# Third chunk of single batches made on ScalarE and its queue; the raw rows' fill moved to the first tap

## The chip, the cores and the metric

The kernel runs on one core of a Trainium2 chip. The core's engines work side by side and each executes its own instructions in order: TensorE (PE; weight loads are listed as PEld), VectorE (DVE), ScalarE (ACT), GpSimd (POOL) and SyncE (SP). The last three also issue DMA transfers, each from a queue of its own. The metric is the device time of one execution in microseconds, lower is better; the median of several runs is compared.

## The reference

For 8 batches of 4096 tokens with 192 features, a causal convolution with 7 softmax taps (one set per head of 24 features), then a token-mixing and a channel-mixing MLP, each with a residual:

```
w = softmax(weight)                                   # 8 heads x 7 taps
x[b,s,h,g] = sum_k w[h,k] * x_pad[b,s+k,h,g]          # 6 zero rows ahead of each batch
h  = relu(xT @ w_tok1) @ w_tok2                       # over the tokens: 4096 -> 256 -> 4096
u  = x + hT
out = u + relu(u @ w_ch1) @ w_ch2                     # over the features: 192 -> 1536 -> 192
```

Everything is float32. The kernel gets its products by splitting a factor into a high part, rounded to the matmul's format, and a low part, the rest.

## The kernel before

**Groups and tiles.** The batches run in five groups: batch 0, batch 1, then the pairs 2 and 3, 4 and 5, 6 and 7. A batch is eight tiles of 512 tokens. For each tile `mix2` makes u, the convolution's output plus the token mix; then the channel MLP runs in two halves, `channel1` (products with w_ch1, line 1228) and `channel2` (products with w_ch2, lines 1308 and 1309, then the sums into osb, lines 1314 and 1315). After each pair of products of `channel1`, ScalarE writes the relu's high part hh (line 1271) and VectorE its low part hl (line 1272); the next products of `channel2` need both.

**The hand-over of a tile.** `channel1` needs the tile's u with features on the partitions. In the two single batches `transposed_once` does that for the next tile, in the middle of `channel2` of the present one. 192 features are three chunks of 64 features; each tile has its two token halves on the two halves of the 128 partitions, and the tile's pieces are dealt so that TensorE's transposes fill two of three chunks (c = 0 and 1) of each half, one PSUM tile of 128x512 each. ScalarE copies such a tile to own_hi (line 1156), and VectorE subtracts the copy from the same PSUM tile and writes own_lo (line 1157). The third chunk of a partition half is a copy of one of the other half's chunks, so four transfers of 128 KB, issued by GpSimd, carry it across the partitions: two for own_hi and then two for own_lo (lines 1159 and 1160). `channel1` multiplies the chunks 0 and 1 first, high and low parts, and the third chunk's last:

```
prods = [(w, v, c) for cs in (range(ND - 1), [ND - 1]) for w, v in order for c in cs]
```

`transposed_once` runs 14 times, for the tiles 1 to 7 of batch 0 and 0 to 6 of batch 1, between 112 and 564 us. The pairs of batches use other functions.

**Work of later batches.** Beside that runs stage 1 of the groups to come. `load` fetches raw rows of x on SP's queue and, for the first tile of a batch (q2 = 0), fills the 6 rows ahead of it with zeros on GpSimd (line 809). `taps` makes the convolution head by head: the first tap is ScalarE's and writes xc (line 817), the other six are VectorE's and add to it (line 819). xc goes to xcd in DRAM from GpSimd's queue (line 853). For batch 0's second token weights, ScalarE casts the decoded weights to stage (line 1432), and SP stores them to t2d (line 1434); the buffer of stage must be stored before it is written again.

**What sets the order.** The program is written out once, and each engine executes in the order of writing. An object `bg` holds streams of stage-1 work; the foreground's calls of `bg.fg(pe, dve)` tell it the cost of what was just written, and it places as much stage-1 work between as its estimates allow. Waits between engines are set by a framework that follows the tiles which instructions read and write.

Of the kernel before, what the change touches and what calls it, by code (L numbers as in the profile page):

```python
# [142 lines left out]
def conv_mixer_kernel(ctx: ExitStack, tc: tile.TileContext, x, weight, w_tok1, w_tok2, w_ch1, w_ch2, out):  # L143
    nc = tc.nc
# [10 lines left out]
    ND = D // D2  # L155
# [5 lines left out]
    HALO = K - 1  # L161
# [8 lines left out]
    def f32(ap):  # L170
        return ap.bitcast(F32)
# [612 lines left out]
    def stage1(gi, pools):  # L784
# [13 lines left out]
        def load(q2, part):  # L798

            ds = slice(part * DH, (part + 1) * DH)  # L800
            raw = pools(part).tile([P, RB + HALO, nb, DH], F32, name=f"raw{part}")
            for i, b in enumerate(bs):

                at = (b * S + q2 * ST - HALO) * D + ds.start
                assert at >= 0
                src = bass.AP(tensor=x.tensor, offset=x.offset + at, ap=[[RB * D, P], [D, RB + HALO], [1, DH]])
                nc.sync.dma_start(out=raw[:, :, i, :], in_=src)
                if q2 == 0:
                    nc.gpsimd.memset(raw[0:1, 0:HALO, i, :], 0.0)
            return raw  # L810

        def conv(raw, xc, h, k):
# [26 lines left out]
        def taps(q2, h, k):  # L839
            st = states[q2]  # L840
            if k == 0 and h == 0:
                if done.get(("storing", q2 - 2)):
                    bg.release()
                st["xc"] = pools(q2 % 2).tile([P, RB * nb, D], F32, name=f"xc{q2 % 2}")
            for i in range(2):
                conv(st["raw", h // HH], st["xc"], h + i, k)

# [298 lines left out]
    def transposed_once(u):  # L1146

        own = own_tile("hi"), own_tile("lo")
        low, high = slice(0, D2), slice(D2, P)
        for c in range(ND - 1):  # L1150
            ps = ps_x.tile([P, TT], F32, name="ps_x")
            for j in range(TJ):
                cols = u[:, j].rearrange("p c b d -> p (c b d)")[:, c * D2:(c + 2) * D2]
                nc.tensor.transpose(out=ps[:, j * P:(j + 1) * P], in_=cols, identity=ident)
            bg.fg(440, 600)
            nc.scalar.copy(out=own[0][:, c], in_=ps)
            nc.vector.tensor_tensor(out=own[1][:, c], in0=ps, in1=f32(own[0][:, c]), op=ALU.subtract)
        for k in range(2):
            nc.gpsimd.dma_start(out=f32(own[k][high, ND - 1]), in_=f32(own[k][low, 0]))
            nc.gpsimd.dma_start(out=f32(own[k][low, ND - 1]), in_=f32(own[k][high, ND - 2]))  # L1160
        return [(own, own, [range(ND), [(c + 1) % ND for c in range(ND)]])]

    def blocks_sent(z, place):

# [137 lines left out]
    def channel2(i, h, u, osb, js, at=None):  # L1302
        for j in js:
            ts = slice(j * P, (j + 1) * P)
            ps = ps_x.tile([P, TT], F32, name="ps_x")
            for n, f in enumerate(order):
                z = n == NF - 1
                nc.tensor.matmul(out=ps[:, :2 * D], lhsT=h["hh", f][:, ts], rhs=w2[:, f, :], start=n == 0, stop=False)  # L1308
                nc.tensor.matmul(out=ps[:, :D], lhsT=h["hl", f][:, ts], rhs=w2[:, f, :D], start=False, stop=z)  # L1309
                if n % 4 == 3:  # L1310
                    bg.fg(1140, 660 if z else 0, 200)
                if at and at[0] == (j, n):
                    at[1]()
            nc.vector.tensor_tensor(out=rows(osb[:, j]), in0=rows(ps[:, :D]), in1=tokens(u, i)[:, j], op=ALU.add)
            nc.vector.tensor_tensor(out=osb[:, j], in0=ps[:, D:2 * D], in1=osb[:, j], op=ALU.add)  # L1315
# [133 lines left out]
    for gi, bs in enumerate(GROUPS):  # L1449
# [13 lines left out]
        for q in range(NT):  # L1463
            nxt = (gi, q + 1) if q + 1 < NT else (gi + 1, 0)
            for i, b in enumerate(bs):
# [73 lines left out]
                if ahead:  # L1539
                    product2(i, h, u, osb, half[0])  # L1540
                if turn and not pairs and ahead:
                    abc = transposed_once(loaded[1])
                run_ahead(gi)
                if last and q + 1 == NT and i + 1 == nb:
                    for j in range(TJ):
                        if j in half[1]:
                            channel2(i, h, u, osb, [j])
                        store_out(gi, b, q, osb, range(j, j + 1), nc.sync)
                else:
                    if ahead:  # L1550
                        if turn and pairs:
                            made = []
                            channel2(i, h, u, osb, half[1], ((half[1][0], 7), lambda: made.extend(parted(other[:, 1], other))))
                            abc = made
                        else:
                            product2(i, h, u, osb, half[1])
                    else:
                        made = []
                        first_channel2(u, osb, [3], (NF // 3, lambda: made.extend(transposed(loaded[1]))))
                        abc = made  # L1560
                        second_split()
                        first["parted"] = 0.0
                        bg.dve = max(bg.dve, bg.pe) + 6e3

                    store_out(gi, b, q, osb, range(TJ), nc.gpsimd if ahead else nc.scalar)
# [38 lines left out]
```

## Time and profile before

| | us |
|---|---|
| median of 3 runs | 2014.27 |
| lowest and highest of them | 2013.43, 2015.42 |
| profiled execution, its own time | 2013.42 |
| span of the profile | 2011.7 |
| TensorE busy | 1999.8 |
| VectorE busy | 1507.3 |
| ScalarE busy | 749.1 |
| GpSimd busy | 241.6 |

The span is what the profiler recorded, from the first to the last instruction; the execution's own time has 1.7 us around it. Busy times are sums over one engine's instructions, so they lie beside each other in time. A start time in the trace is counted from the beginning of the span.

### The profile page before, as it was taken

How to read it: one execution, taken by the hardware profiler on the slowest of the kernel's cores; microseconds unless marked ns; L12 is line 12 of the kernel's file. 1: busy time of each engine (PE TensorE's matmuls, PEld its weight loads, DVE VectorE, ACT ScalarE, POOL GpSimd, SP SyncE). 2: the span in 40 equal slices, each digit the busy share in tenths (PEclk: the TensorE clock that was granted, in tenths of full speed). 3: DMA queues.
4: the chain of work that ended last, by engine and by line, in shares of the span. 5: the costliest groups of instructions: out<-in, count | busy, mean ns of one | idle time of the engine just before them, and what ended most of it. 6: DMA issues, size and time to landing. Idle time of an engine off the chain costs nothing.

```text
span 2011.7 us, 45407 instructions
## 1 busy us (share of the span) xinstructions
PE 1999.8 (99%) x19007; PEld 1856.2 (92%) x19007; DVE 1507.3 (75%) x3022; ACT 749.1 (37%) x1252; POOL 241.6 (12%) x431
## 2 busy tenths in 40 slices
PE   9999999999999999999999999999999999999999
PEld 9899989998999999999999999999999999999998
DVE  6899989999559999757888789456666666666664
ACT  6666433433333343323334433333233322333322
POOL 1010111111111101111101110111111110111110
PEclk9999999999999999999999999999999999999999
DMA  9957456664454467425346544533323222333310
GB/s 305 307 169 230 147 174 198 191 178 159 149 157 131 141 181 204 149 65 139 76 135 176 153 119 122 139 87 85 85 61 80 75 64 64 84 85 85 85 48 17
DMA packets 284481, 266.61 MB, mean 133 GB/s; under 512 B 190980, under 2 KB 232516, under 8 KB 284276
## 3 DMA queue, kind: packets, MB, share of 16 engines
q1 hardware_dynamic: 258404, 172.85, 30.7%
q0 software_dynamic: 25344, 90.47, 15.1%
q8 instruction: 150, 2.46, 0.5%
q14 instruction: 55, 0.45, 0.1%
q10 hardware_dynamic: 528, 0.39, 0.1%
HBM read 147.25 MB, written 71.30 MB: 109 GB/s over the span
## 4 chain that ended last, share of the span: by engine, by line
PE 92%; DMA 3%; DVE 2%; ACT 1%; SPq 1%; issue 0%; POOL 0%; POOLq 0%; ACTq 0%; DVEq 0%
PE ps_x L1228 38%; PE ps_x L1289 26%; PE ps_x L1308 10%; PE ps_x L1309 5%; PE ps_x L1110 3%; PE ps_a L925 2%; PE ps_a L926 2%; PE ps_a L927 2%; PE ps_x L1080 1%; PE ps_a L921 1%; PE ps_x L1083 1%; DMA x<-in_x_dram 1%; DMA t1d<-kept_t 1%; PE ps_x L1085 1%; PE ps_x L1084 1%; DMA dec_raw<-in_moe_w_tok_dram 1%
## 5 line engine op out<-in xcount | busy, mean ns | idle before, releaser
L1271 ACT ACTIVATE hh<-ps_x 128x512 fp32r<-128x512 f32 x756 | 410.4, 596 | 859.8 <-PE ps_x L1228 859.8
L1272 DVE SCALAR_TENSOR_TENSOR hl<-ps_x,hh 128x512 fp32r<-128x512 f32 x756 | 484.2, 683 | 177.6 <-ACT hh L1271 176.7
L1289 PE MATMUL ps_x<-w,hh 64*128 64x384 f32 x3648 | 523.3, 355 | 0.0
L1289 PE MATMUL ps_x<-w,hl 64*128 64x192 f32 x3648 | 460.7, 247 | 0.0
L1228 PE MATMUL ps_x<-other,w_hi 64*128 64x512 f32 x1728 | 448.3, 388 | 0.1
L819 DVE SCALAR_TENSOR_TENSOR xc<-raw,cw,xc 128x384 f32<-128x384 f32 (+1 forms) x768 | 388.3, 559 | 11.9 <-ACT xc L817 11.8
L1289 PEld LDWEIGHTS ps_x<-w,hl 64*128 64x128 f32 x3648 | 355.8, 188 | 1.8 <-DVE hl L1272 0.3
L1228 PE MATMUL ps_x<-own_hi,w_hi 64*128 64x512 f32 x1440 | 348.0, 392 | 3.6 <-DVE osb L1315 2.0
L1289 PEld LDWEIGHTS ps_x<-w,hh 64*128 64x128 f32 x3648 | 349.7, 184 | 1.4
L1308 PE MATMUL ps_x<-w,hh 128*128 128x384 f32 x1200 | 348.2, 361 | 0.0
L1228 PEld LDWEIGHTS ps_x<-other,w_hi 64*128 64x128 f32 x1728 | 315.7, 184 | 31.8 <-DVE hl L1272 0.4
L1228 PE MATMUL ps_x<-own_lo,w_hi 64*128 64x512 f32 x1440 | 341.7, 387 | 1.3 <-DMA own_lo<-own_lo 1.3
L1228 PE MATMUL ps_x<-own_hi,w_lo 64*128 64x512 f32 x1440 | 341.8, 387 | 0.0
L1309 PE MATMUL ps_x<-w,hl 128*128 128x192 f32 x1200 | 300.6, 250 | 0.0
L1228 PEld LDWEIGHTS ps_x<-own_hi,w_hi 64*128 64x128 f32 x1440 | 214.2, 184 | 33.6 <-issue 6.6
L1228 PEld LDWEIGHTS ps_x<-own_lo,w_hi 64*128 64x128 f32 x1440 | 218.7, 184 | 26.4 <-DMA own_lo<-own_lo 1.7
L1228 PE MATMUL ps_x<-other,w_lo 64*128 64x512 f32 x864 | 242.1, 387 | 0.0
L1228 PEld LDWEIGHTS ps_x<-own_hi,w_lo 64*128 64x128 f32 x1440 | 218.7, 184 | 25.0
L1309 PEld LDWEIGHTS ps_x<-w,hl 128*128 128x128 f32 x1200 | 229.6, 191 | 0.0
L1308 PEld LDWEIGHTS ps_x<-w,hh 128*128 128x128 f32 x1200 | 225.3, 188 | 0.5 <-DVE hl L1272 0.4
L1297 DVE TENSOR_TENSOR osb<-ps_x,osb 128x192 f32<-128x192 f32 x456 | 162.9, 357 | 26.4
L1228 PEld LDWEIGHTS ps_x<-other,w_lo 64*128 64x128 f32 x864 | 159.2, 184 | 16.4
(187 smaller groups left out, 2016.8 us busy)
## 6 DMA issues: line engine op xcount, KB each, us to landing
raw<-in_x_dram SPq DMA_DIRECT2D x56, 672.0 KB, 7.6
t<-t2d SPq DMA_DIRECT2D x64, 512.0 KB, 5.4
out_dram<-osb POOLq DMA_DIRECT2D x62, 384.0 KB, 4.3
xcd<-xc POOLq DMA_DIRECT2D x28, 768.0 KB, 8.4
u<-xcd SPq DMA_DIRECT2D x56, 384.0 KB, 5.7
t<-t1p SPq DMA_DIRECT2D x32, 512.0 KB, 5.9
other<-own_hi POOLq DMA_DIRECT2D x24, 384.0 KB, 3.9
other<-own_lo POOLq DMA_DIRECT2D x24, 384.0 KB, 3.8
```

What stands on the lines that cost most here:

```text
L819: nc.vector.scalar_tensor_tensor(out=dst, in0=src, scalar=cw[:, h, k:k + 1], in1=dst, op0=ALU.mult, op1=ALU.add)
L925: nc.tensor.matmul(out=ps, lhsT=wh, rhs=xh, start=a, stop=False)
L926: nc.tensor.matmul(out=ps, lhsT=wh, rhs=xl, start=False, stop=False)
L927: nc.tensor.matmul(out=ps, lhsT=wl, rhs=xh, start=False, stop=z)
L1110: nc.tensor.matmul(out=ps[:, :n], lhsT=t2[ks, kc, r, j, :], rhs=h1[ks, kc, v, :n], start=m == 0, stop=m == len(prods) - 1)
L1228: nc.tensor.matmul(out=ps, lhsT=w1[w][rows, chunks[h][c], p * P:(p + 1) * P], rhs=t[h][v][rows, c], start=n == 0, stop=n == len(prods) - 1,)
L1271: nc.scalar.activation(out=h["hh", f], in_=ps, func=AF.Relu)
L1272: nc.vector.scalar_tensor_tensor(out=h["hl", f], in0=ps, scalar=0.0, in1=f32(h["hh", f]), op0=ALU.max, op1=ALU.subtract)
L1289: nc.tensor.matmul(out=ps[:, :m], lhsT=h[part, f][ks, ts], rhs=w2[ks, f, :m], start=n == 0 and part == "hh", stop=z and part == "hl",)
L1297: nc.vector.tensor_tensor(out=osb[:, j], in0=v, in1=osb[:, j], op=ALU.add)
L1308: nc.tensor.matmul(out=ps[:, :2 * D], lhsT=h["hh", f][:, ts], rhs=w2[:, f, :], start=n == 0, stop=False)
L1309: nc.tensor.matmul(out=ps[:, :D], lhsT=h["hl", f][:, ts], rhs=w2[:, f, :D], start=False, stop=z)
```

## The change

Three things change. First, in `transposed_once` ScalarE copies the third chunk's part of own_hi out of PSUM: after each chunk's subtraction a copy of 64 partitions by 512, from one partition half of the PSUM tile to the other half of own_hi. Secondly, the two transfers that carry the third chunk's part of own_lo are put into a function `rest`, which `channel2` calls after product n = 7 of its second half's first column block, and they are issued from ScalarE's queue. GpSimd issues none of the four transfers any more. Thirdly, the fill of the raw rows leaves `load` and stands in `taps`, directly ahead of ScalarE's first tap of each half of the heads, and fills both batches of a pair at once.

```diff
@@ load
                 nc.sync.dma_start(out=raw[:, :, i, :], in_=src)
-                if q2 == 0:
-                    nc.gpsimd.memset(raw[0:1, 0:HALO, i, :], 0.0)
             return raw
@@ taps
+            if k == 0 and q2 == 0 and h % HH == 0:
+                nc.gpsimd.memset(st["raw", h // HH][0:1, 0:HALO], 0.0)
             for i in range(2):
                 conv(st["raw", h // HH], st["xc"], h + i, k)
@@ transposed_once
             nc.scalar.copy(out=own[0][:, c], in_=ps)
             nc.vector.tensor_tensor(out=own[1][:, c], in0=ps, in1=f32(own[0][:, c]), op=ALU.subtract)
-        for k in range(2):
-            nc.gpsimd.dma_start(out=f32(own[k][high, ND - 1]), in_=f32(own[k][low, 0]))
-            nc.gpsimd.dma_start(out=f32(own[k][low, ND - 1]), in_=f32(own[k][high, ND - 2]))
-        return [(own, own, [range(ND), [(c + 1) % ND for c in range(ND)]])]
+            src, dst = (high, low) if c else (low, high)
+            nc.scalar.copy(out=own[0][dst, ND - 1], in_=ps[src])
+
+        def rest():
+            for c, (src, dst) in enumerate(((low, high), (high, low))):
+                nc.scalar.dma_start(out=f32(own[1][dst, ND - 1]), in_=f32(own[1][src, c]))
+
+        return [(own, own, [range(ND), [(c + 1) % ND for c in range(ND)]])], rest
@@ the tile loop
-                    abc = transposed_once(loaded[1])
+                    abc, rest = transposed_once(loaded[1])
+                        elif turn:
+                            channel2(i, h, u, osb, half[1], ((half[1][0], 7), rest))
```

The order of the instructions on TensorE, VectorE and SP stays as it was. ScalarE's is shown at the hand-over at 288 us (the sixth, of tile 6 of batch 0 to tile 7), with the waits that each instruction has; hh and xc are the relu's high part and the convolution's output, h is the token MLP's. Before:

```order
L1271 ACTIVATE hh_2966<-ps_x 128x512 [waits PE_49] x2
L817 ACTIVATE xc_3125<-raw_2943,cw 128x16x24 x2
L1156 CAST own_hi<-ps_x 128x512 [waits DMASW7_49,DMASW0_49,PE_49]
L1156 CAST own_hi<-ps_x 128x512 [waits PE_49]
L433 ACTIVATE h_479<-ps_a_775 128x192
L433 ACTIVATE h_479<-ps_a_776 128x192
```

The same place of the changed kernel:

```order
L1275 ACTIVATE hh_2964<-ps_x 128x512 [waits PE_49] x2
L815 ACTIVATE xc_3123<-raw_2943,cw 128x16x24 x2
L1156 CAST own_hi<-ps_x 128x512 [waits PE_49]
L1159 CAST own_hi<-ps_x 64x512 [waits DVE_49]
L1156 CAST own_hi<-ps_x 128x512 [waits PE_49]
L1159 CAST own_hi<-ps_x 64x512 [waits DVE_49]
L1163 DMA own_lo<-own_lo 64x512 [waits DMAHW5_49,DMAHW3_49]
L1163 DMA own_lo<-own_lo 64x512
L433 ACTIVATE h_479<-ps_a_775 128x192
L433 ACTIVATE h_479<-ps_a_776 128x192
```

Each chunk's copy is followed by a copy of 64 partitions that waits for VectorE, and two transfers of own_lo stand behind the second of them. At the hand-overs of the first two and of the eleventh, one or two casts stand between those copies and the transfers.

GpSimd's order at the fill of the first pair's rows (raw_2943; xcd and out_dram are stores to DRAM). Before:

```order
L1159 DMA own_hi<-own_hi 64x512
L1160 DMA own_hi<-own_hi 64x512
L1159 DMA own_lo<-own_lo 64x512
L1160 DMA own_lo<-own_lo 64x512
L809 MEMSET raw_2943 1x6x96 x2
L1322 DMA out_dram<-osb 128x4x192
L853 DMA xcd_76<-xc_2807 128x1536
```

The same place of the changed kernel:

```order
L853 DMA xcd_76<-xc_2395 128x1536
L1326 DMA out_dram<-osb 128x4x192
L853 DMA xcd_76<-xc_2807 128x1536
L844 MEMSET raw_2943 1x1152
L1326 DMA out_dram<-osb 128x4x192
L844 MEMSET raw_3375 1x1152
```

The fill has moved behind an output store and the store of xc_2807 to xcd, is one instruction in place of two, and no own_hi or own_lo transfer is left on this queue.

## Rows read from the trace of the kernel before

**Rows 1.** Page: busy time of each engine, share of span, instructions.

```profile
PE 1999.8 (99%) x19007; PEld 1856.2 (92%) x19007; DVE 1507.3 (75%) x3022; ACT 749.1 (37%) x1252; POOL 241.6 (12%) x431
```

**Rows 2.** Waits of TensorE: waiting group, releaser, us in all, times, longest.

```profile
PE ps_x L1228 <- DVE osb L1315: 2.0, 1, 2.0
...
PE ps_x L1228 <- DMA own_lo<-own_lo: 1.3, 1, 1.3
```

**Rows 3.** Chain that ended last, in time: start us, length us, what.

```profile
244.27 10.40 DMA t2d<-stage
...
257.49 2.74 DVE xc L819 x8
...
448.41 7.84 DMA own_lo<-own_lo
```

**Rows 4.** Lines 1156, 1157: ns of one (least/median/most), first to last start, shape.

```profile
L1156 ACT CAST own_hi<-ps_x x28: 565/588/597, 115.5 to 548.8; 128x512 fp32r<-128x512 f32 x28
```
L1157 DVE TENSOR_TENSOR own_lo<-ps_x,own_hi x28: 678/680/692, 116.1 to 549.5; 128x512 fp32r<-128x512 f32 x28
```

**Rows 5.** Timeline at hand-over 1: start us, us, engine, line, operation, out<-in.

```profile
115.51 1.05 ACT L1156 CAST own_hi<-ps_x 128x512 fp32r<-128x512 f32 x2
...
116.45 0.63 ACT L240 CAST t2s<-dec_top 128x512 fp32r<-128x512 f32 x1
...
116.97 1.21 ACT L1432 CAST stage<-t2s 128x512 fp32r<-128x512 f32 x1
...
122.59 0.39 PE L1228 MATMUL ps_x<-own_lo,w_hi 64*128 64x512 f32 x2
```

**Rows 6.** ScalarE's issue (line 1322), landing of line 1159's transfers, median landing of t2d.

```profile
L1322 ACTq DMA_DIRECT2D out_dram<-osb x1: 411/411/411, 93.8 to 93.8; - x1
...
DMA to landing us min/median/max: 2.1/2.6/7.8
...
t2d<-stage SPq DMA_DIRECT2D x16, 512.0 KB, 4.6
```

**Rows 7.** Timeline at hand-over 2.

```profile
143.91 1.22 ACT L1432 CAST stage<-t2s 128x512 fp32r<-128x512 f32 x1
...
144.93 1.28 DVE L1157 TENSOR_TENSOR own_lo<-ps_x,own_hi 128x512 fp32r<-128x512 f32 x2
145.02 0.68 ACT L199 ACTIVATE dec_top<-dec_raw 128x512 f32<-128x512 f32 x1
...
152.04 0.39 PE L1228 MATMUL ps_x<-own_lo,w_hi 64*128 64x512 f32 x2
```

**Rows 8.** Timeline ahead of hand-over 4: VectorE's pair of hl, TensorE's next products.

```profile
226.29 1.28 DVE L1272 SCALAR_TENSOR_TENSOR hl<-ps_x,hh 128x512 fp32r<-128x512 f32 x2
...
227.75 0.63 PE L1228 MATMUL ps_x<-own_hi,w_hi 64*128 64x512 f32 x4
```

**Rows 9.** Timeline at hand-over 5.

```profile
242.12 1.07 ACT L1156 CAST own_hi<-ps_x 128x512 fp32r<-128x512 f32 x2 [5.01 <-issue]
...
243.08 1.17 ACT L1432 CAST stage<-t2s 128x512 fp32r<-128x512 f32 x1
...
244.04 1.28 DVE L1157 TENSOR_TENSOR own_lo<-ps_x,own_hi 128x512 fp32r<-128x512 f32 x2
```

**Rows 10.** Line 809's fill as in rows 4, then the timeline around hand-over 6.

```profile
L809 POOL MEMSET raw<- x14: 567/569/575, 99.0 to 927.9; 1x576 f32 x14
...
271.23 0.54 POOL L853 DMA_DIRECT2D xcd<-xc  x1 [5.04 <-DVE xc L819]
...
272.06 1.14 DVE L819 SCALAR_TENSOR_TENSOR xc<-raw,cw,xc 128x384 f32<-128x384 f32 x2
...
289.88 1.28 DVE L1157 TENSOR_TENSOR own_lo<-ps_x,own_hi 128x512 fp32r<-128x512 f32 x2
...
294.88 0.41 PE L1228 MATMUL ps_x<-own_lo,w_hi 64*128 64x512 f32 x2
```

**Rows 11.** Timeline at hand-over 11, VectorE.

```profile
446.84 1.28 DVE L1157 TENSOR_TENSOR own_lo<-ps_x,own_hi 128x512 fp32r<-128x512 f32 x2
```

## The prediction

> **What bounds the kernel now.** I read the busy times first. TensorE is busy for 1999.8 us of a span of 2011.7, VectorE for three quarters of it, ScalarE for 37% and GpSimd for 12% [rows 1]. So work taken off GpSimd is worth nothing by itself. What can be won is a gap on TensorE, and what can be lost is a new one. The waits of TensorE come next: in `channel1` only two are over 1 us, one of 2.0 us put down to VectorE and one of 1.3 us for a transfer of own_lo [rows 2]. The chain of waits says what lies behind each [rows 3]. The 2.0 us end a line that begins with the store of stage to t2d at 244.27: 10.40 us in transit, then ScalarE's casts, then VectorE's taps late at 257.49. The 1.3 us end the last of the four transfers of a hand-over (the copying of the third chunk into place, done 14 times between 112 and 564 us), issued at 448.41 and 7.84 us on its way. I number the hand-overs 1 to 14.
>
> The profiled execution took 2013.42 us, its span 2011.7 and 1.7 around it. The sum is made against it; the median of the three runs shown lies 0.85 above.
>
> **The two copies on ScalarE.** Each hand-over now has four ScalarE copies instead of two, and the built order shows that each new copy waits for VectorE: for the subtraction that reads the same PSUM tile. VectorE's second subtraction needs ScalarE's third copy, which stands behind that waiting one. So the engines go in turns. A copy takes 0.59 us and a subtraction 0.68 [rows 4]; of two copies back to back the second adds about 0.48, since a pair takes 1.05 [rows 5]; a 64-partition copy has the same 512 elements a partition, and I give it the same. Before, the subtractions end 0.59 + 1.28 = 1.87 us after the first copy starts. Now they end after 0.59 + 0.68 + 0.59 + 0.48 + 0.68 = 3.02, so VectorE loses about 1.1 us a hand-over, and the last copy ends after 3.61, so ScalarE is held 2.5 us longer. Where VectorE comes to its first subtraction late, at D, the last copy ends at D + 3.02.
>
> No row of before has two engines in one PSUM tile at once: the first subtraction of all, on the same tile as the first copy, starts at 116.1, and that copy, of 0.59, at 115.5 [rows 4]. Were the new copy and the subtraction side by side, VectorE would lose nothing, and the terms of hand-overs 1 to 4 below, 3.9 us, would go. The Trainium skill ("PSUM — Partial Sum Buffer", section "PSUM bank collisions raise a hardware error") says that two engines in one bank and one 32-partition quadrant at once raise an error, a read beside a read included, and that the compiler therefore adds a dependency between them. By that rule the built wait cannot be dropped and speaks against this change; the trace, which shows no overlap of that kind, agrees as far as it goes.
>
> **own_lo's transfers on ScalarE's queue.** An issue there costs 0.41 us of ScalarE; GpSimd's issues of these transfers land after 2.1 to 7.8 us, median 2.6, and I take 2.6 for the new ones [rows 6]. They are not earlier than before: they stand behind the copies and, at some hand-overs, behind casts that ScalarE owes to the stage for later batches. Hand-over by hand-over:
>
> Hand-over 1: the first copy starts at 115.51, the last ends 3.61 later at 119.12; two casts of 0.63 and 1.21 follow (together to 118.18 before, so 1.7), to 120.8; issues at 120.8 and 121.2; landing at 123.8. TensorE wants this half of own_lo at 122.59 [rows 5]. Loss 1.2 (0.7 at a landing of 2.1).
>
> Hand-over 2: VectorE reaches the subtraction at 144.93, last copy at 147.95; two ScalarE steps of 1.22 and 0.68 (1.8 together) to 149.7; landing at 150.1 + 2.6 = 152.7 against 152.04 [rows 7]. Loss 0.7 (0.2 at 2.1).
>
> Hand-overs 3 and 4: here no transfer is short, but VectorE is. Ahead of hand-over 4 its pair of hl ends at 226.29 + 1.28 = 227.57, and TensorE goes on at 227.75, 0.18 later [rows 8]. If 1.1 us is pushed through, 0.9 is lost; hand-over 3 is alike, up to 1.1. Together 2.0, from 0.
>
> Hand-over 5 is where the 10.40 us store leaves. ScalarE starts at 242.12, VectorE at 244.04, so the last copy ends at 247.06, and the cast to stage (1.17, now at 243.08) ends at about 248.2, 3.9 us later than at 244.25 [rows 9]. If the store still takes 10.40, everything behind it, to TensorE's gap, is 3.9 later. If it takes 4.6, the median of its kind [rows 6], it lands at 252.8 instead of 254.67, 1.9 earlier. The new issue time lies past two of the four hand-over transfers that went along with it, which speaks for a shorter one, and there are loads of t beside it, which do not. I take the middle, +1.0, and keep both ends.
>
> **The raw fill.** The fill of the first rows is 0.57 us on GpSimd [rows 10] and stood early, at the load. Now it stands behind the queue's earlier issues and right ahead of ScalarE's first tap. Eight stay of fourteen; a pair's is one over twice the elements, between 0.57 and 1.14. At hand-over 6 GpSimd is at an issue that it makes when VectorE is done: 271.23 + 0.54 = 271.77, then the fill to 272.3 to 272.9, then a tap, taken at 0.57 like each of VectorE's products of that shape. VectorE's first product behind that tap starts at 272.06 [rows 10], so VectorE is 0.9 to 1.4 late; I take 0.9. The subtraction, at 289.88, then starts at 290.8, the last copy ends at 293.8, issues follow at 293.8 and 294.2, landing at 296.8 against a want at 294.88: loss 1.9 (0.5 if VectorE has caught up and landing is 2.1; 2.4 with the longer fill). The three other pair groups start where GpSimd is freer: 0.3 for all, 0 to 0.6.
>
> **The 7.84 us transfer.** At hand-over 11 VectorE is at 446.84, so last copy 449.86, one cast of 0.63 like that of [rows 5], issues at 450.5 and 450.9, landing at 453.5. Before, the last transfer landed at 448.41 + 7.84 = 456.25 and TensorE had waited 1.3, which puts the want at about 455.0 [rows 2, 3, 11]: the 1.3 us go. With 7.84 again it lands at 458.7, 2.4 later than now. I take +0.5. At the seven hand-overs left (7 to 10, 12 to 14) the waits name no shortage; I take 0, bounded by hand-over 1's 0.7 each, 4.9.
>
> GpSimd's 56 issues of some 0.5 us (0.54 for the one of [rows 10]) that go are beside TensorE in all places but these; nothing for them.
>
> **The sum.** 1.2 + 0.7 + 2.0 + 1.0 + 1.9 + 0.3 + 0.5 = 7.6 us. On the profiled execution 2021.0, on the median 2021.9: 2022.0.
>
> **The rivals.** (A) Not slower: transfers at their medians. With two transfers a hand-over instead of four in flight, the store of hand-over 5 takes 4.6 (−1.9, not +1.0) and hand-over 11 lands in 2.6 (−1.3, not +0.5): 7.6 − 2.9 − 1.8 = 2.9, or 2017.2 on the median; with landings at 2.1 at hand-overs 1, 2 and 6 and no loss at hand-over 3 it is about 0. It decides at hand-over 5: at a store under 254.67 − 248.2 = 6.5 us that place gains, and from about 5.7 down, with hand-over 11, the sum is inside the measurement. For it: [rows 6] put 10.40 at over twice the median. Against: the first two transfers were not the store's only company. (B) The change's wait does not bite because copy and subtraction end up apart anyway, VectorE being late: then only the fill and the store stay, about 2014 to 2015. Against: at hand-over 1 VectorE subtracts at once, 0.6 us behind the copy [rows 4]. (C) A gain: both waits of [rows 2] go, 2.0 + 1.3 = 3.3, and nothing takes their place: 2011. Against: hand-overs 1, 2 and 6 have no cover. (D) Much slower: the store at 10.40 (+2.9 over what I took) and 0.7 to 1.2 at each of the seven hand-overs left: 7.6 + 2.9 + 4.9 to 8.4, or 2029.7 to 2033.
>
> **How the numbers follow.** Forecast 0.60, A 0.18, B 0.05, C 0.05, D 0.12. Likeliest 2022.0. The range leaves out C, the lower part of A and B and the upper part of D: 2014.5 to 2031.0. A measurement of this kernel can tell about 0.2%, 4.0 us, from no change: faster is C, 0.05; within it are A and B but for a little of A's upper end, 0.20; slower is the rest, 0.75.
>
> **What would show it.** In the profile after: the rows of the two GpSimd transfer lines gone; 28 copies of 64x512 on ScalarE, each pair with a wait for VectorE's subtraction; VectorE's subtraction waiting for ScalarE about 1.1 us a hand-over, 15 us in all; TensorE waiting for own_lo at hand-overs 1, 2 and 6 (0.7 to 1.9 each), and for VectorE near 227; the gap near 261 moved with the store's transit. I am wrong if the subtractions follow each other as before, if own_lo lands early although issued late, or if TensorE's idle time does not rise by 5 to 10 us. A fall at 456 with none of the new waits would be A or C.

## The result and the profile after

The changed kernel took 2025.18 us (median of 6 runs, 2022.62 to 2027.11) against 2013.69 for the kernel before beside it: 11.5 us slower, a ratio of 1.0056 with a 95% interval of 1.0043 to 1.0069. The forecast was 2022.0, slower, with a range of 2014.5 to 2031.0. The profiled execution of the changed kernel has a span of 2023.7 us, 12.0 more than before.

The busy times on the page after, which answer to [rows 1]:

```profile
PE 2006.3 (99%) x19007; PEld 1859.0 (92%) x19007; DVE 1508.7 (75%) x3022; ACT 768.2 (38%) x1280; POOL 212.4 (10%) x369
```

GpSimd has lost 29 us of work and nobody gained by it. VectorE does the same work as before; TensorE has the same 19007 products, is "busy" 6.5 us longer and idle 5.5 us longer (17.4 against 11.9). The waits after, first TensorE's, which answer to [rows 2], then VectorE's and ScalarE's around the third chunk (waiting group, releaser, us in all, times, longest):

```profile
PE ps_x L1232 <- DMA own_lo<-own_lo: 6.1, 3, 2.4
PE ps_x L1232 <- DVE osb L1319: 1.5, 1, 1.5
...
PE ps_x L1232 <- DVE hl L1276: 0.7, 3, 0.3
...
DVE own_lo L1157 <- ACT own_hi L1156: 18.3, 16, 1.3
...
ACT own_hi L1159 <- DVE own_lo L1157: 31.5, 28, 5.7
```

All 28 new copies wait for VectorE, and VectorE waits for ScalarE 18.3 us at its subtractions, where the kernel before had 1.3 in all:

```profile
DVE own_lo L1157 <- ACT own_hi L1156: 1.3, 4, 0.5
```

TensorE waits 6.1 us for own_lo instead of 1.3. Hand-over 2 shows the whole chain (timeline after, columns as in [rows 5]):

```profile
145.91 0.68 DVE L1157 TENSOR_TENSOR own_lo<-ps_x,own_hi 128x512 fp32r<-128x512 f32 x1
146.62 0.58 ACT L1159 CAST own_hi<-ps_x 64x512 fp32r<-64x512 f32 x1 [2.29 <-DVE own_lo L1157]
147.23 0.59 ACT L1156 CAST own_hi<-ps_x 128x512 fp32r<-128x512 f32 x1
147.85 0.69 DVE L1157 TENSOR_TENSOR own_lo<-ps_x,own_hi 128x512 fp32r<-128x512 f32 x1 [1.26 <-ACT own_hi L1156]
148.57 0.59 ACT L1159 CAST own_hi<-ps_x 64x512 fp32r<-64x512 f32 x1 [0.76 <-DVE own_lo L1157]
...
149.49 0.61 ACTq L1163 DMA_DIRECT2D own_lo<-own_lo  x1
...
154.77 0.50 PE L1232 MATMUL ps_x<-own_lo,w_hi 64*128 64x512 f32 x2 [1.78 <-DMA own_lo<-own_lo]
...
158.54 0.84 PE L1232 MATMUL ps_x<-own_hi,w_hi 64*128 64x512 f32 x4
```

Subtraction, copy, copy, subtraction, copy, each behind the one before it: the turns. The second transfer is issued at 149.49 and TensorE's product waits for it until 154.77, 5.3 us later. The same product stood at 152.04 before [rows 7]. The last line shows what comes on top. Before, that product started here:

```profile
154.30 0.62 PE L1228 MATMUL ps_x<-own_hi,w_hi 64*128 64x512 f32 x4
```

So the stretch from the awaited product to this one took 2.26 us before and 3.77 after, with nothing to wait for in it. The stretches of the trace after (start:end, us, then busy time of PE, PEld, DVE, ACT, POOL, the granted TensorE clock, the DMA engines' busy share, GB/s) say why:

```profile
152.00:154.80 2.80, 1.02 (x12) 0.51 (x8) 2.73 (x8) 1.72 (x3) 0.71 (x1) 1.00 0.97 340
...
156.00:157.00 1.00, 1.00 (x8) 0.81 (x6) 0.55 (x1) 1.00 (x3) 0.00 (x0) 0.50 0.99 387
...
159.00:160.00 1.00, 1.00 (x12) 0.84 (x10) 0.59 (x1) 1.00 (x3) 0.00 (x0) 1.00 0.78 303
```

The granted clock was 0.50, the lower of the two levels (1.2 of 2.4 GHz), for about 3 us behind the wait, and eight products went where twelve fit at full clock. In the stretch before, while the transfer was on its way, the DMA column has 0.97: the DMA engines were busy with more than this transfer. That this made it late is argued, not shown.

Hand-over 11 repeats this, issue, wait and clock:

```profile
459.33 1.33 ACTq L1163 DMA_DIRECT2D own_lo<-own_lo  x1
...
466.57 0.79 PE L1232 MATMUL ps_x<-own_lo,w_hi 64*128 64x512 f32 x2 [2.39 <-DMA own_lo<-own_lo]
...
469.91 0.40 PE L1232 MATMUL ps_x<-own_hi,w_lo 64*128 64x512 f32 x2
...
467.00:468.00 1.00, 1.00 (x6) 0.72 (x6) 1.00 (x3) 0.60 (x2) 0.00 (x0) 0.50 1.04 406
```

The same two products before, where the transfer was awaited too:

```profile
456.30 0.50 PE L1228 MATMUL ps_x<-own_lo,w_hi 64*128 64x512 f32 x2 [1.29 <-DMA own_lo<-own_lo]
...
458.24 0.40 PE L1228 MATMUL ps_x<-own_hi,w_lo 64*128 64x512 f32 x2
```

They were 1.94 us apart, and are 3.34 apart now. What the half clock adds to the whole time is not shown by this: the one of the six runs of the changed kernel whose mean granted clock was 1.000 took 2024.86 us, the profiled one, with two such stretches and a mean of 0.998, took 2025.50.

### The profile page after: what moved, and what is told of

It is laid out like the page before. It is cut to its first block, busy times and chain, and to the rows that moved or that the text cites. A ratio compares the mean times of both kernels' runs of the same rounds, so it can differ in the third digit from the quotient of the medians.

```text
span 2023.7 us, 45362 instructions
## 1 busy us (share of the span) xinstructions
PE 2006.3 (99%) x19007; PEld 1859.0 (92%) x19007; DVE 1508.7 (75%) x3022; ACT 768.2 (38%) x1280; POOL 212.4 (10%) x369
## 4 chain that ended last, share of the span: by engine, by line
PE 53%; DVE 0%; ACT 0%; issue 0%
PE ps_x L1232 23%; PE ps_x L1293 22%; PE ps_x L1110 3%; PE ps_x L1312 2%; PE ps_x L1313 1%; PE ps_a L925 1%; PE ps_a L926 1%; PE ps_a L927 1%; PE ps_x L1083 0%; PE ps_x L1085 0%; PE ps_x L1084 0%; DVE xc L817 0%; DVE hl L1276 0%; ACT xc L815 0%; DVE osb L1318 0%; DVE osb L1319 0%
## 5 line engine op out<-in xcount | busy, mean ns | idle before, releaser
L1276 DVE SCALAR_TENSOR_TENSOR hl<-ps_x,hh 128x512 fp32r<-128x512 f32 x756 | 484.4, 686 | 174.2 <-ACT hh L1275 173.4
L1293 PE MATMUL ps_x<-w,hl 64*128 64x192 f32 x3648 | 465.9, 247 | 0.3 <-DVE hl L1276 0.3
L1232 PE MATMUL ps_x<-other,w_hi 64*128 64x512 f32 x1728 | 448.1, 388 | 0.1
L817 DVE SCALAR_TENSOR_TENSOR xc<-raw,cw,xc 128x384 f32<-128x384 f32 (+1 forms) x768 | 389.1, 562 | 12.3 <-ACT xc L815 12.3
L1293 PEld LDWEIGHTS ps_x<-w,hl 64*128 64x128 f32 x3648 | 367.6, 188 | 2.1 <-DVE hl L1276 0.8
L1293 PEld LDWEIGHTS ps_x<-w,hh 64*128 64x128 f32 x3648 | 362.1, 184 | 1.4
L1232 PE MATMUL ps_x<-own_hi,w_hi 64*128 64x512 f32 x1440 | 352.2, 394 | 3.5 <-DVE osb L1319 1.5
L1232 PE MATMUL ps_x<-own_lo,w_hi 64*128 64x512 f32 x1440 | 345.6, 389 | 6.1 <-DMA own_lo<-own_lo 6.1
L1232 PE MATMUL ps_x<-own_hi,w_lo 64*128 64x512 f32 x1440 | 345.1, 388 | 0.0
L1232 PEld LDWEIGHTS ps_x<-other,w_hi 64*128 64x128 f32 x1728 | 315.2, 184 | 29.9 <-DVE hl L1276 0.4
L1313 PE MATMUL ps_x<-w,hl 128*128 128x192 f32 x1200 | 300.4, 250 | 0.0
L1232 PEld LDWEIGHTS ps_x<-own_lo,w_hi 64*128 64x128 f32 x1440 | 220.6, 185 | 33.7 <-DMA own_lo<-own_lo 7.9
L1232 PEld LDWEIGHTS ps_x<-own_hi,w_hi 64*128 64x128 f32 x1440 | 216.0, 185 | 36.2 <-issue 5.6
L1232 PEld LDWEIGHTS ps_x<-own_hi,w_lo 64*128 64x128 f32 x1440 | 220.3, 185 | 26.0
L1232 PE MATMUL ps_x<-other,w_lo 64*128 64x512 f32 x864 | 242.0, 386 | 0.0
L1313 PEld LDWEIGHTS ps_x<-w,hl 128*128 128x128 f32 x1200 | 229.1, 191 | 0.0
L1232 PEld LDWEIGHTS ps_x<-other,w_lo 64*128 64x128 f32 x864 | 159.0, 184 | 15.5
## 6 DMA issues: line engine op xcount, KB each, us to landing
t<-t2d SPq DMA_DIRECT2D x64, 512.0 KB, 5.3
t<-t1p SPq DMA_DIRECT2D x32, 512.0 KB, 5.4
```

The source lines that it names most:

```text
L817: nc.vector.scalar_tensor_tensor(out=dst, in0=src, scalar=cw[:, h, k:k + 1], in1=dst, op0=ALU.mult, op1=ALU.add)
L1232: nc.tensor.matmul(out=ps, lhsT=w1[w][rows, chunks[h][c], p * P:(p + 1) * P], rhs=t[h][v][rows, c], start=n == 0, stop=n == len(prods) - 1,)
L1276: nc.vector.scalar_tensor_tensor(out=h["hl", f], in0=ps, scalar=0.0, in1=f32(h["hh", f]), op0=ALU.max, op1=ALU.subtract)
L1293: nc.tensor.matmul(out=ps[:, :m], lhsT=h[part, f][ks, ts], rhs=w2[ks, f, :m], start=n == 0 and part == "hh", stop=z and part == "hl",)
```

## The experiments

Two theories stood at first. "Turns": the loss is ScalarE and VectorE going in turns. "Queue": it is own_lo's transfers on ScalarE's queue at a later point. A third, "fill", puts it on the moved fill. All differences below are between medians, against the kernel before that ran beside each; their 95% intervals reach some 1.8 us to either side, and up to 2.6 where a kernel ran fewer than ten times. So the difference of two such differences is known to some 2.5 to 3.6 us.

**Each part alone, and the turns undone.** First the fill alone (the diff's hunks in `load` and `taps`):

> The kernel before with the raw rows' fill alone moved to the first tap; hand-overs as before. Theory 'turns' (the loss of 11.5 us comes from ScalarE's copies standing between VectorE's subtractions, which makes the two engines go in turns): +0.3 to +1.5 us over the kernel before, because the fill alone can delay only VectorE's products behind it, and VectorE must then make TensorE wait on its own. Rival 'fill' (VectorE comes 1.4 us later to hand-over 6 and to the pair groups behind it, and the waits there stem from that): +2.5 to +4 us, with a wait of TensorE for own_lo at hand-over 6. Rival 'queue' says as 'turns' here.

Measured: 2015.07 against 2014.24, +0.8 us, ratio 1.0005 (0.9996 to 1.0014). On its own the fill costs nothing that can be told, as "turns" had it.

Then the copies alone:

```diff
             nc.vector.tensor_tensor(out=own[1][:, c], in0=ps, in1=f32(own[0][:, c]), op=ALU.subtract)
-        for k in range(2):
-            nc.gpsimd.dma_start(out=f32(own[k][high, ND - 1]), in_=f32(own[k][low, 0]))
-            nc.gpsimd.dma_start(out=f32(own[k][low, ND - 1]), in_=f32(own[k][high, ND - 2]))
+            src, dst = (high, low) if c else (low, high)
+            nc.scalar.copy(out=own[0][dst, ND - 1], in_=ps[src])
+        nc.gpsimd.dma_start(out=f32(own[1][high, ND - 1]), in_=f32(own[1][low, 0]))
+        nc.gpsimd.dma_start(out=f32(own[1][low, ND - 1]), in_=f32(own[1][high, ND - 2]))
```

> The kernel before with the two copies of the third chunk's high part on ScalarE, each behind its chunk's subtraction as in the changed kernel; own_lo's two transfers stay on GpSimd's queue, directly behind, and the fill stays at the load. Theory 'turns': +6 to +10 us, waits of TensorE for own_lo at hand-overs 2 and 11 again, VectorE's subtraction waiting for ScalarE about 1.2 us at each hand-over. Rival 'queue' (the loss comes from own_lo's transfers standing in ScalarE's queue at a later point of the program): within 2 us of the kernel before. Rival 'fill': +7 to +9.

Measured: 2017.17 against 2014.24, +2.9 us, 1.0015 (1.0006 to 1.0024). VectorE waited for ScalarE 18.3 us as in the changed kernel, but the time was half of what "turns" asked for, and none of TensorE's waits for own_lo (2.0 us in all) was at hand-over 2.

Then the queue alone:

```diff
-        for k in range(2):
-            nc.gpsimd.dma_start(out=f32(own[k][high, ND - 1]), in_=f32(own[k][low, 0]))
-            nc.gpsimd.dma_start(out=f32(own[k][low, ND - 1]), in_=f32(own[k][high, ND - 2]))
+        nc.gpsimd.dma_start(out=f32(own[0][high, ND - 1]), in_=f32(own[0][low, 0]))
+        nc.gpsimd.dma_start(out=f32(own[0][low, ND - 1]), in_=f32(own[0][high, ND - 2]))
+        def rest():
+            for c, (src, dst) in enumerate(((low, high), (high, low))):
+                nc.scalar.dma_start(out=f32(own[1][dst, ND - 1]), in_=f32(own[1][src, c]))
```

> The kernel before with own_lo's two transfers alone moved to ScalarE's queue and to the later point of the program; own_hi's two transfers stay on GpSimd's queue, the fill at the load. Theory 'turns': -1 to +2 us, because the subtractions end as early as before and ScalarE's queue is free then. Rival 'queue': +6 to +10 us. Rival 'fill': within 2 us.

Measured: 2017.45 against 2014.24, +3.2 us, 1.0014 (1.0005 to 1.0023). Between the two expectations: neither theory had it.

And the changed kernel without the turns:

```diff
             nc.vector.tensor_tensor(out=own[1][:, c], in0=ps, in1=f32(own[0][:, c]), op=ALU.subtract)
-            src, dst = (high, low) if c else (low, high)
-            nc.scalar.copy(out=own[0][dst, ND - 1], in_=ps[src])
+            tiles.append(ps)
+        for c, (src, dst) in enumerate(((low, high), (high, low))):
+            nc.scalar.copy(out=own[0][dst, ND - 1], in_=tiles[c][src])
```

> The changed kernel with the two copies of the third chunk placed behind both subtractions instead of one behind each; own_lo's transfers on ScalarE's queue and the fill as in the changed kernel. Theory 'turns': 7 to 11 us faster than the changed kernel, so 0 to +4 over the kernel before; VectorE's waits for ScalarE at the subtractions back to some 1 to 4 us in all. Rivals 'queue' and 'fill': at most 4 us faster than the changed kernel, so +7.5 or more over the kernel before.

Measured: 2017.04 against 2014.24, +2.8 us, 1.0013 (1.0004 to 1.0022); VectorE's waits at the subtractions are 0.7 us in all, as "turns" had it. Undoing the turns alone takes back some 8.7 of the 11.5 us, though the turns alone had cost 2.9. The three parts alone came to 0.8 + 2.9 + 3.2 = 6.9. So either the parts make each other worse, or one of them hides a gain.

**Which of the two.** A new pair of theories: "late landing" (each part delays own_lo, and all eat the same slack ahead of the same waits), and "busy engines" (VectorE and ScalarE come late to their own work, whatever the transfers do). First the copies behind both subtractions, with GpSimd issuing own_lo's two transfers at once and the fill at the load:

```diff
-        for k in range(2):
-            nc.gpsimd.dma_start(out=f32(own[k][high, ND - 1]), in_=f32(own[k][low, 0]))
-            nc.gpsimd.dma_start(out=f32(own[k][low, ND - 1]), in_=f32(own[k][high, ND - 2]))
+            tiles.append(ps)
+        for c, (src, dst) in enumerate(((low, high), (high, low))):
+            nc.scalar.copy(out=own[0][dst, ND - 1], in_=tiles[c][src])
+        nc.gpsimd.dma_start(out=f32(own[1][high, ND - 1]), in_=f32(own[1][low, 0]))
+        nc.gpsimd.dma_start(out=f32(own[1][low, ND - 1]), in_=f32(own[1][high, ND - 2]))
```

> The kernel before with the third chunk's high part copied by ScalarE behind both subtractions; own_lo's two transfers on GpSimd's queue directly behind, where own_hi's no longer stand ahead of them; the fill at the load. Theory 'late landing' (the time lost in the changed kernel is mainly TensorE's wait for own_lo at a few hand-overs, and the half clock behind the longest of these waits; each part of the change issues own_lo later, and the parts add up because each eats the same slack): own_lo leaves about 1 us earlier than in the kernel before, so -3 to +0.5 us against it, the wait for own_lo at hand-over 11 shorter. Rival 'busy engines' (VectorE and ScalarE come later to their own work, whatever the transfers do): +1 to +3 us, from two more copies on ScalarE at each hand-over.

Measured: 2011.74 against 2014.12, 2.4 us faster, 0.9986 (0.9977 to 0.9995). This is the hidden gain: ScalarE's copies are worth having, in this place. It is also the version that beats both kernels. The reason expected for it does not hold: hand-over 11 of this kernel has

```profile
446.39 1.07 ACT L1157 CAST own_hi<-ps_x 128x512 fp32r<-128x512 f32 x2 [10.21 <-PE ps_x L1155]
...
449.01 0.53 POOL L1164 DMA_DIRECT2D own_lo<-own_lo  x1
```

so that own_lo's last transfer leaves 2.62 us behind the first copy, where before it was 2.67 (445.74 to the 448.41 of [rows 3]). In this trace the waits that answer to [rows 2] are shorter by 1.0 us together:

```profile
PE ps_x L1232 <- DVE osb L1319: 1.4, 1, 1.4
...
PE ps_x L1232 <- DMA own_lo<-own_lo: 0.9, 1, 0.9
```

Two of four transfers of a hand-over are gone there. Where the 2.4 us come from stays open, and this trace cannot tell it: the profiled execution was the slowest of the eleven and took 2013.45 us, as long as the one of before with its 2013.42.

The changed kernel with own_lo's transfers back on GpSimd's queue, at once, and so with turns and fill:

> The changed kernel with own_lo's two transfers back on GpSimd's queue directly behind the copies (so without the move to ScalarE's queue). Parts that simply add (0.8 of the fill, 2.9 of the copies): 2018 us, +3.7 over the kernel before. Theory 'late landing': as much, +3 to +5, since GpSimd issues as soon as VectorE's second subtraction ends. Rival 'busy engines': +7 or more, since the queue alone gave only 3.2 and the turns and the fill must carry the rest of the 11.5.

Measured: 2019.98 against 2014.12, +5.9 us, 1.0028 (1.0016 to 1.0039), between the two. The changed kernel with the fill back at the load, and so with turns and queue:

> The changed kernel with the fill back at the load. Parts that simply add (2.9 of the copies, 3.2 of the queue): +6.1 over the kernel before. Theory 'late landing': more than the sum, +8 to +11, since copies and queue delay the same transfer; waits of TensorE for own_lo of 2 us and more at hand-overs 2 and 11, each with a stretch of half clock behind it. Rival 'fill' (the fill's 1.4 us of VectorE at hand-over 6 is what the others do not have): +6 or less.

Measured: 2023.17 against 2014.12, +9.0 us, 1.0043 (1.0031 to 1.0056), inside what "late landing" expected. Its places fit less well: at hand-over 2 TensorE waited 1.6 us for own_lo and the granted clock stayed at 1.00; half clock came at hand-over 11, behind a wait of 2.6 us, and at 267.66, behind a wait of 1.8 us for VectorE. Then the wait itself was taken away:

```diff
-                    out=ps, lhsT=w1[w][rows, chunks[h][c], p * P:(p + 1) * P], rhs=t[h][v][rows, c], start=n == 0,
+                    out=ps, lhsT=w1[w][rows, chunks[h][c], p * P:(p + 1) * P],
+                    rhs=t[h][v][rows, 0 if len(t) > 2 and v and c == ND - 1 else c], start=n == 0,
```

> The changed kernel, but the products of own_lo's third chunk read its first chunk instead, so that TensorE waits for no transfer of own_lo; the transfers themselves and everything on the other engines stay. This changes part of what is computed. Theory 'late landing': the 6.1 us of waits and some 2.5 to 3 us of half clock go: 2016 to 2018 us, 7 to 9 us faster than the changed kernel; the granted clock is full at hand-overs 2 and 11. Rival 'busy engines': at most 4 us faster, new waits of TensorE for VectorE or for own_hi take the place.

Measured: 2022.30 against 2014.12, +8.2 us, 1.0044 (1.0031 to 1.0056): only some 3 us faster than the changed kernel, with a granted clock of 1.00 through all hand-overs of its trace. That is what "busy engines" allowed; "late landing" as the main cause falls. The waits of TensorE in this kernel, and the place of the longest:

```profile
PE ps_x L1313 <- DVE hl L1277: 1.8, 2, 1.3
...
PE ps_x L1232 <- DVE hl L1277: 1.0, 4, 0.5
...
310.25 1.05 POOL L844 MEMSET raw<- 1x1152 f32 x1 [9.77 <-DMA raw<-in_x_dram]
311.33 1.13 ACT L815 ACTIVATE xc<-raw,cw 128x384 f32<-128x384 f32 x2 [2.23 <-POOL raw L844]
312.36 1.06 ACT L1276 ACTIVATE hh<-ps_x 128x512 fp32r<-128x512 f32 x2
...
312.97 1.29 DVE L1277 SCALAR_TENSOR_TENSOR hl<-ps_x,hh 128x512 fp32r<-128x512 f32 x2 [3.03 <-ACT hh L1276]
...
313.72 0.44 PE L1313 MATMUL ps_x<-w,hh 128*128 128x384 f32 x1 [1.30 <-DVE hl L1277]
```

Where own_lo no longer holds TensorE up, hl does. Here it is the moved fill: 1.05 us between the raw load's landing and ScalarE's tap, the tap ahead of ScalarE's relu, the relu ahead of VectorE's hl. The changed kernel has no wait of TensorE at this place: TensorE comes to the same product only at 316.29, having waited for own_lo further ahead. The same kernel with the fill at the load:

> The changed kernel with the products of own_lo's third chunk reading its first chunk (TensorE waits for no transfer of own_lo; this changes part of what is computed), and with the fill back at the load. What is left is the turn-taking of ScalarE and VectorE and the empty transfers. Theory 'VectorE is a second bound' (between 100 and 500 us VectorE has hardly a free stretch, so each 1.2 us that a hand-over makes it stand still reaches TensorE as a late hl where no transfer holds TensorE longer): +4 to +7 us over the kernel before, waits of TensorE for hl in place of those for own_lo; the wait of 1.3 us behind the pair's fill is gone. Rival 'late landing' (what matters is the transfers, and the waits for hl come from the fill): 0 to +2.

Measured: 2019.97 against 2013.58, +6.4 us, 1.003 (1.002 to 1.004), as "VectorE is a second bound" had it. The view of waits lists for hl 1.3 us in 5 places together and 0.5 in a sixth, but TensorE loses more there than it lists: two products that stood at 225.48 and 227.75 before, 2.27 us apart, stand at 229.59 and 233.57 here, 3.98 apart, and of the 1.7 us between the view lists 0.5. Counted over the trace by every product that starts as the hl it waits for is ready, against the same product of before, the pauses for hl come to about 7 us in this kernel, to 3 with the copies alone, and to nothing with the copies behind both subtractions. The trace of before shows why VectorE has so little to give (stretches, columns as above):

```profile
100.00:200.00 100.00, 100.00 (x768) 92.90 (x765) 94.18 (x225) 65.96 (x105) 9.99 (x17) 1.00 0.63 200
200.00:300.00 100.00, 97.72 (x717) 91.00 (x718) 88.86 (x222) 37.36 (x69) 11.35 (x20) 1.00 0.52 158
...
400.00:500.00 100.00, 98.71 (x736) 93.11 (x736) 93.48 (x187) 34.18 (x61) 13.07 (x23) 1.00 0.55 170
```

Over the span VectorE is busy 75% of the time, but between 100 and 500 us, where all but two of the hand-overs lie, it is 89 to 94%.

**Queue or place.** Three kernels differ from the fastest one only in who issues own_lo's transfers, and where. On ScalarE's queue at the later point:

> The changed kernel with ScalarE's copies behind both subtractions and the fill at the load; own_lo's transfers stay on ScalarE's queue at the later point. Beside the run with the same copies and GpSimd's queue (2.4 us faster than the kernel before) this tells what the queue alone costs where there are no turns. Theory 'VectorE is a second bound' with landing on top: 0 to +2.5 us over the kernel before, one wait of 1 to 2 us for own_lo at hand-over 11 or 6. Rival 'queue' (the later point of issue costs as much with turns or without): +3.5 to +6.

Measured: 2016.74 against 2013.58, +3.2 us, 1.0014 (1.0006 to 1.0023), between the two, nearer to "queue". On ScalarE's queue directly behind the copies (`nc.scalar` for `nc.gpsimd` in the two transfers of the fastest):

> ScalarE's copies behind both subtractions, the fill at the load, and own_lo's two transfers on ScalarE's queue, but directly behind the copies instead of at the later point. With GpSimd's queue at this place the kernel was 2.4 us faster than the kernel before, with ScalarE's queue at the later point 3.2 us slower. Theory 'queue' (an issue on ScalarE's queue lands later and holds ScalarE's own next step, wherever it stands): +2 to +5 us over the kernel before. Rival 'point' (the place further down the program is what costs): -3 to 0 us.

Measured: 2015.13 against 2013.60, +1.5 us, 1.0010 (1.0001 to 1.0019), again between the two and nearer to "queue". On GpSimd's queue at the later point (`nc.gpsimd` for `nc.scalar` in `rest`):

> ScalarE's copies behind both subtractions, the fill at the load, and own_lo's two transfers at the later point of the program, but on GpSimd's queue. Theory 'queue': -3 to 0 us against the kernel before. Rival 'point': +2 to +5 us.

Measured: 2013.24 against 2013.60, -0.4 us, 0.9999 (0.9990 to 1.0008). As "queue" had it: ScalarE's queue costs about 3.6 to 3.9 us at either place; the later point costs about 2 on either queue, which is less than can be told. By the median the transfers land no later. The median landings of own_lo's transfers at the same early place (KB each, us) are, for the fastest kernel and then for the one on ScalarE's queue,

```profile
own_lo<-own_lo POOLq DMA_DIRECT2D x28, 128.0 KB, 2.7
...
own_lo<-own_lo ACTq DMA_DIRECT2D x28, 128.0 KB, 2.6
```

But the transfer that TensorE waits for does: at hand-over 11 the last one landed after 8.1 us from ScalarE's queue and 7.5 from GpSimd's, and TensorE waited 1.8 us against 0.9. At the later point the clock comes in as well. On ScalarE's queue the four of eleven runs with a mean granted clock of 1.000 have a median of 2014.84 us and the seven with 0.999 one of 2017.64; on GpSimd's queue all eleven have 1.000. The profiled execution on ScalarE's queue, one of the seven, is at half clock for 3.4 us behind a wait of 1.87 us for own_lo at hand-over 11.

ScalarE itself differs too. Its idle time for which the profile shows no releaser, listed as "issue", in the kernel on ScalarE's queue at the early place:

```profile
ACT stage L1436 <- issue: 2.7, 3, 1.5
ACT t L889 <- issue: 2.1, 3, 0.7
ACT xc L817 <- issue: 1.3, 2, 0.7
```

With two places of 0.6 more these are ten, 7.3 us in all, and in the timeline each stands right behind the second issue of a hand-over. With GpSimd's queue ScalarE has one, of 1.1 us, at 1203 us, behind no such issue. At the later point on ScalarE's queue they come to 2.1 us only, where the queue costs nearly as much. So late landing, the clock and ScalarE held at its issues all show in these traces; how the 3.6 to 3.9 us divide among them stays open.

**The account.** With the fill at the load, in us against the kernel before:

| | GpSimd's queue, at once | ScalarE's queue, later |
|---|---|---|
| copies behind both subtractions | -2.4 | +3.2 |
| a copy behind each subtraction (turns) | +2.9 | +9.0 |

The turns cost 5.3 in one column and 5.8 in the other, the queue with its later point 5.6 and 6.1. As far as the intervals let one tell, these two simply add, and both are clear of them. On top of both the fill costs 11.5 - 9.0 = 2.5 (and 5.9 - 2.9 = 3.0 with turns alone), but 0.8 on its own and -0.4 without turns (2.8 against 3.2); that it costs more with turns is within the intervals and not shown. So the change is -2.4 + 5.3 + 5.6 + 2.5 = 11.0 of the 11.5 measured. Alone, the copies seemed to cost 2.9 because their own gain of 2.4 was in it.

## Why the prediction was right, and which of its steps were not

The direction and the range held, and so did the two causes named, turns and late own_lo; the size was put at 8.3 us over the median before the change (2022.0 against 2013.69) and was 11.5. What the sum had wrong is how the causes share the time: it gave most to late landings, while 8.2 of the 11.5 us stay when TensorE waits for no own_lo. By place, from rows of before and after of the same product of TensorE:

```profile
122.96 0.39 PE L1232 MATMUL ps_x<-own_lo,w_hi 64*128 64x512 f32 x2
...
234.08 0.73 PE L1232 MATMUL ps_x<-own_hi,w_hi 64*128 64x512 f32 x3
...
266.98 0.70 PE L1232 MATMUL ps_x<-own_hi,w_hi 64*128 64x512 f32 x3 [1.49 <-DVE osb L1319]
...
303.26 0.50 PE L1232 MATMUL ps_x<-own_lo,w_hi 64*128 64x512 f32 x2 [1.92 <-DMA own_lo<-own_lo]
```

They stood at 122.59 [rows 5], 227.75 [rows 8], 261.04 (where the 2.0 us of [rows 2] end) and 294.88 [rows 10] before. With 154.30 to 158.54 and 458.24 to 469.91 from above, TensorE's lag goes 0.37, 4.24, 6.33, 5.94, 8.38, 11.67 and 12.0 at the end.

| place | forecast | measured |
|---|---|---|
| hand-over 1 | +1.2 | no wait, 0.37 lag at most |
| hand-over 2 | +0.7 | +3.9 |
| hand-overs 3 and 4 | +2.0 | +2.1 |
| hand-over 5, the store | +1.0 | -0.4 |
| hand-over 6, with the fill | +1.9 | +2.4 |
| hand-overs 7 to 11 | +0.5 | +3.3 |
| the rest | +0.3 | +0.3 |

That the sum came out as near as it did is partly luck: hand-overs 1 and 5 were put 2.2 us too high, hand-overs 2 and 7 to 11 were put 6.0 too low. The column tells where TensorE lost its time in this kernel, not what would come back if one of the waits were gone.

**The turns** were right, in kind and in size: 18.3 us of VectorE's waiting against 15 forecast, copies of 0.58 us; the second of two copies in a row adds 0.61 (146.62 to 147.23) and not 0.48. The experiment that moves the copies behind both subtractions shows that they cost 5.3 to 5.8 us of the 11.5, each known to some 3. The rule of the Trainium skill weighed there ("PSUM — Partial Sum Buffer", "PSUM bank collisions raise a hardware error") held as far as a trace can show it: all 28 copies waited for the subtraction of their tile. It does not follow that the copies must cost: behind both subtractions they wait as well and the kernel is faster. Rival B falls with it.

**Hand-overs 3 and 4** agree in the sum, and in part by luck. At hand-over 4 TensorE waits for VectorE's hl as forecast, and from the product at 230.31 (225.48 before) to the one at 234.08 its lag grows by 1.5 us, where 0.9 was put. From 158.54 to 230.31, with hand-over 3, the lag grows by 0.6, where 1.1 was put, and the view lists no wait of TensorE for hl there.

**Hand-over 1** failed at the step "issues stand behind casts". ScalarE's rows there (after):

```profile
118.72 0.58 ACT L1159 CAST own_hi<-ps_x 64x512 fp32r<-64x512 f32 x1 [0.76 <-DVE own_lo L1157]
118.73 0.51 ACTq L1163 DMA_DIRECT2D own_lo<-own_lo  x1
119.20 0.62 ACT L240 CAST t2s<-dec_top 128x512 fp32r<-128x512 f32 x1
119.27 0.60 ACTq L1163 DMA_DIRECT2D own_lo<-own_lo  x1
119.73 1.21 ACT L1436 CAST stage<-t2s 128x512 fp32r<-128x512 f32 x1
```

Both casts are written ahead of the issues, and yet the first issue starts before either and the second before the longer one. The Trainium skill ("PSUM — Partial Sum Buffer", section "Engine vs sequencer instructions") says that what the sequencer does itself, a nop or a semaphore operation, waits only until earlier instructions have been dispatched to the engine, not until they are complete. It does not name DMA issues there; these rows show the same of two. The 1.2 us of this term were never there.

**Hand-overs 2 and 11** failed at the landing and at what a wait brings with it. I took 2.6 us; it was 5.3 (149.49 to 154.77) and 7.2 (459.33 to 466.57). The 2.6 was the median of line 1159's transfers, half of which carry own_hi; own_lo's alone had a median of 3.4 us before and have 3.1 after. And the last transfers of these two hand-overs had been 3.9 and 7.8 us on their way in the kernel before, so each place's own landing would have told more than any median. At hand-over 11 the far end that I had kept, 7.84, is near what came. And no term held the half clock behind a long wait: 3.77 - 2.26 = 1.5 us and 3.34 - 1.94 = 1.4 us, 2.9 together in the profiled execution.

**Hand-over 5** came out between its ends. ScalarE's cast waits for the store of stage (after):

```profile
254.91 0.32 SPq L1438 DMA_DIRECT2D t2d<-stage  x1
...
260.69 1.23 ACT L1436 CAST stage<-t2s 128x512 fp32r<-128x512 f32 x1 [2.98 <-DMA t2d<-stage]
```

That is 5.8 us in transit, under the 6.5 from which that place gains. Rival A had this half right; its other half, hand-over 11 at the median landing, did not come.

**Hand-over 6** was near. The pair's fill took 1.05 us, inside its bounds, and VectorE's first product behind it:

```profile
277.72 1.05 POOL L844 MEMSET raw<- 1x1152 f32 x1
278.80 1.12 ACT L815 ACTIVATE xc<-raw,cw 128x384 f32<-128x384 f32 x2 [3.47 <-POOL raw L844]
279.45 1.15 DVE L817 SCALAR_TENSOR_TENSOR xc<-raw,cw,xc 128x384 f32<-128x384 f32 x2 [1.37 <-ACT xc L815]
```

It starts at 279.45 against 272.06 [rows 10], 7.4 later where TensorE is 5.9 later: VectorE 1.4 us behind, the upper end of 0.9 to 1.4.

**Queue.** "Nothing earlier than before" was right, but I charged ScalarE's queue through the landings alone. Of the queue's 6.1 us with turns (9.0 against 2.9), taking away TensorE's wait for the transfers returned 2.6 (9.0 to 6.4). The other 3.5 came with TensorE waiting for no own_lo at all; they reach it by VectorE's hl, for which TensorE pauses some 4 us more in that trace than in the one of the copies alone. How much of them is ScalarE held at an issue stays open.

## What to carry to other kernels

Ahead of adding an instruction, look at whom it waits for and who is queued behind it: the same two copies gave 2.4 us when they stood behind both of VectorE's subtractions and cost 2.9 when they stood between them. Read an engine's busy share for the stretch in question (89 to 94% here), not for the span (75%); VectorE, nearly full there, acted as a second bound, and taking away the wait one saw uncovered the one behind it. Take a transfer's landing from its own place in the trace before (7.8 us at hand-over 11), not from a median (2.6). Parts that seem to make each other worse may be parts of which one hides a gain: a two-by-two table of variants, not each part alone, told that. And see whether the traced execution is a typical one of its kernel: that of the fastest kernel here was its slowest.

## What the runs showed of the hardware

In the changed kernel TensorE's granted clock fell to 0.50, the level of 1.2 GHz, for about 3 us at waits of 1.78 and 2.39 us, and the products behind them took 1.5 and 1.4 us longer than before; it stayed at 1.00 at the wait of 1.92 us at hand-over 6. The length of the wait does not decide it: with the queue alone it fell at a wait of 2.35 us and stayed at 1.00 at one of 2.6. A transfer of 128 KB at the same place of the program landed in 2.6 us (median of 28) from ScalarE's queue and in 2.7 from GpSimd's; at hand-over 11 the last one took 8.1 and 7.5. A DMA issue written behind two casts on ScalarE started ahead of both (118.73 against 119.20), and the next step of ScalarE stood idle behind two issues for 0.6 to 1.5 us in ten of fourteen hand-overs of one kernel.
